# Column sums ahead of the folds of x, a higher credit cap, an eighth pre-split matrix and loads behind gathers in an attention and two-layer MoE kernel

## The chip, the cores and the metric

The kernel runs on one core of a Trainium2 chip. The metric is the time on the device in microseconds, as the median of three executions. TensorE (PE) multiplies, VectorE (DVE) and ScalarE (ACT) work on vectors, GpSimd (POOL) does the same more slowly and also issues gathers and scatters, SyncE (SP) issues most of the other DMAs. Each engine works through a queue of its own in order, and semaphores join them. PEld is the loading of weights into TensorE.

## What is computed

Sparse causal attention (8 global keys, a local window of 96) over q, k, v of 2 x 8 x 768 x 64 gives x, 1536 tokens of 512 values. Two mixture-of-experts layers follow, each with 8 experts of 512 x 1024 and 1024 x 512. In the first, each token goes through each expert, weighted by a matrix P that is balanced in eight rounds of row and column sums; in the second each token goes through the one expert that a greedy assignment gives it.

```python
# layer 1
P = np.exp(logits - logits.max())
for _ in range(8):
    P /= P.sum(1, keepdims=True) + 1e-09
    P /= P.sum(0, keepdims=True) + 1e-09
    P *= N / E
for e in range(E):
    out += P[:, e:e + 1] * (np.maximum(x @ w1[e], 0.0) @ w2[e])
# layer 2: each (token, expert) by falling logit, at most N // E tokens an expert
for e in range(E):
    mask = assigned == e
    out[mask] = np.maximum(x[mask] @ w1[e], 0.0) @ w2[e]
```

## The kernel before

**Numbers.** Each float32 matrix is split into an upper and a lower float16 half (`split_hi` L814 on ScalarE, `split_lo` L817 on VectorE), scaled by a power of two from its largest magnitude, and a product is three float16 matmuls (hi x hi, hi x lo, lo x hi; `mm3`, L868 to L870). A matrix is measured in eight pieces of 128x512, by turns on ScalarE (L882) and VectorE (L1197); `settle` joins them (L1204), a small matmul on TensorE spreads the maximum over the partitions (L134), and VectorE turns it into the scale (L122, L140 to L143).

**Stages.** Attention runs first (to about 155 us). Expert 0's first products (`ph`, L868 to L870, evicted by L861 and L862 on ScalarE and L863 on VectorE) start beside it and go on to 197 us. Meanwhile the eight balancing rounds run: on VectorE row sums, L910 to L913, and the column totals over a partition's tokens, pc (L915); on GpSimd `partition_all_reduce`, the sum of pc over the partitions (L917); on VectorE again L918 to L920. Then come expert 0's second products (`expert_out`, L1459, added into acc by L1464 or L1466 on VectorE with factors from the balanced P), and for each further expert the first products in a form with seven products for eight (`hidden`, L1485) and the second products.

**Folds.** That form needs sums and differences of quarters of x. `fold(tb)`, for each of three blocks of tokens, computes them in six GpSimd instructions (L1105 twice, L1111 four times) into a scratch R, which for the first two blocks lies in chunks 4 to 7 and 8 to 11 of acc, for the third in the buffer of weights; then ScalarE and VectorE convert R (L1119, L1120). The folds are traced behind expert 0's first products, but the compiler's scheduler may issue an instruction of GpSimd as early as its operands are there.

**Streams.** In layer 1 the preparation of weights is laid between the products by hand: generators (`maxima`, `weights`, `folds`, the logits) yield the cost of their next piece on ScalarE, VectorE and GpSimd, and `pump`, called after each few matmuls, grants each engine some credit up to `CAPS`; a piece is issued when the credit of each engine is at least its cost or 0.7, whichever is less. From expert 0's second products to the end of layer 1 (`in_order`) each engine's queue follows the order of tracing. `have` pumps without products where a product needs weights that a stream has not issued yet.

**Layer 2's weights.** Its 16 matrices are all measured in layer 1. The first `NPRE` of them (in the order expert 0 first, expert 0 second, expert 1 first, ...) are also split there and stored in DRAM (`pre`, stores at L1343), and layer 2 fetches them, 2 MB each (`fetch`, L1932); the list of jobs is filled by `some(n)`. The others are made in layer 2 (`make`, L1974): eight loads of 256 KB into a ring of five buffers that lies in acc, each followed by L814 and L817.

**Between the layers** the assignment runs in seven rounds, with held-back products (`held`, L1691, added by `flush`, L1704) in TensorE's gaps. At its end the slot table `inv` is computed, acc is stored to DRAM (xg, L1910), and `load_rows` gathers the rows of two experts at a time by three indirect DMAs on GpSimd's queue (L1942); `turn_rows` transposes them (L1953). For each pair of experts there follow first products, `turn_rows` of the next pair, `load_rows` of the one behind it, `fetch_next(4)`, second products, and the scatter of rows (L1914). Loads of `make` are on SP's queue.

`pin` (`tc.keep_in_program_order`) queues an instruction behind the one traced before it on its engine; `tc.issue_after(ins)` queues what its block traces on the engine of `ins` behind `ins`, without waiting for it to finish.

Of the kernel before, what the change touches and what calls it, by code (L numbers as in the profile page):

```python
# [20 lines left out]
P = 128  # L21
# [21 lines left out]
def tile_sparse_attention_moe_moe(ctx, tc, q, k, v, ng, nl, wg1, w11, w12, wg2, w21, w22, out, taps=None):  # L43
# [809 lines left out]
    S2 = cst.tile([P, 2, E, 2], F32)  # L853
    NPRE = 7

# [52 lines left out]
    for it in range(8):  # L908
# [7 lines left out]
        cs = sml.tile([P, E], F32, name="cs")  # L916
        nc.gpsimd.partition_all_reduce(cs, pc, P, bass_isa.ReduceOp.add)  # L917
        nc.vector.tensor_scalar(cs, cs, 1e-9, float(E) / NT, op0=ALU.add, op1=ALU.mult)  # L918
# [175 lines left out]
    def fold(tb):  # L1094
# [8 lines left out]
        for g in range(2):  # L1103
            yield 0, 0, 4.5
            nc.gpsimd.tensor_tensor(R[g], x[:, 0, KH * g:KH * g + KH], x[:, 1, KH * g:KH * g + KH], op=ALU.add)  # L1105
        a11, a21 = R[0][:, :, :HT], R[0][:, :, HT:]
        a12, a22 = R[1][:, :, :HT], R[1][:, :, HT:]
        for o, u, v, op in ((a22, a21, a22, ALU.add), (a21, a11, a21, ALU.subtract), (a11, a22, a11, ALU.subtract),
                            (a12, a12, a11, ALU.subtract)):
            yield 0, 0, 2.5  # L1110
            nc.gpsimd.tensor_tensor(o, u, v, op=op)  # L1111
        yield None
# [249 lines left out]
    for e in range(1, E - 1):  # L1362
        if e != HB:
            jobs.append(("plain", e, 1))
        jobs.append(("fast", e + 1, 0))
        if e in (2, E - 2):
            jobs.append(("gate", HB if e == 2 else E - 1, 1))
        if e in (1, E - 3):
            jobs.append(("back", HB if e == 1 else E - 1, 1))
        some({2: 1, 4: 3, 6: 2}.get(e, 0))  # L1370
        jobs += [pre.pop() for _ in range(PEEKS.get(e, 0))]
# [27 lines left out]

    credit, CAPS = [0.0, 0.0, 0.0], (2.0, 2.0, 2.0)  # L1400
    GROUP, CHUNK, CYCLE = (0.5, 0.5, 0.6, 3), (0.6, 0.5, 1.1, 3), (0.28, 0.32, 0.6, 3)
# [458 lines left out]
    for n in range(1, NC):  # L1860
# [16 lines left out]
    onep = rawp.tile([P, NC, P], F16, name="raw", bufs=2)  # L1877
    h6 = NC // 2
    nc.vector.tensor_tensor(onep[:, :h6], sp[:, :h6, None].to_broadcast([P, h6, P]),
                            ramp[:, None, :].to_broadcast([P, h6, P]), op=ALU.is_equal)  # L1880
# [84 lines left out]
    def make(e, which):  # L1965
# [4 lines left out]
        for a in range(8):  # L1970
            raw = ring[turn_[0] % len(ring)]
            turn_[0] += 1
            c, h = divmod(a, w.shape[1] // 512)
            nc.sync.dma_start(raw, w[c * P:c * P + P, h * 512:h * 512 + 512])  # L1974
            split(raw, S2[:, which, e], t[:, 0, a * 512:a * 512 + 512], t[:, 1, a * 512:a * 512 + 512])
# [86 lines left out]
```

## Time and profile before

| | |
|---|---|
| median of three executions | 1324.1 us (1322.67 to 1326.08) |
| the profiled execution | 1324.13 us, its span 1322.3 us |
| TensorE busy | 1245.2 us, 94% of the span |
| VectorE busy | 889.4 us, 67% |
| ScalarE busy | 754.1 us, 57% |
| GpSimd busy | 207.0 us, 16% |
| mean granted clock of TensorE | 0.984 |
| bytes moved by DMA | 207.19 MB, 157 GB/s |

The profile comes from one execution; times in it are microseconds from the start of its span, means are nanoseconds. A row of the timeline gives start, duration, engine, line, operation, what is written and read with its shape, a count, and in brackets the idle time of the engine before it and what ended that. The granted clock is the share of TensorE's full speed (2.4 GHz) that it was given.

### The profile page before, as it was taken

What the parts mean: (1) busy time and instruction counts of PE and PEld (TensorE: products, weight loads), DVE (VectorE), ACT (ScalarE), POOL (GpSimd) and SP (SyncE); (2) the same over time, 40 slices, a digit from 0 to 9 for tenths busy, and PEclk for the clock granted to TensorE, in tenths of its full rate; (3) what the DMA queues carried; (4) which work ended last, traced back from release to release, by engine and by line L of the source; (5) the groups of instructions that cost most, each with busy time, mean ns of one, the idle gap of its engine ahead of it and who ended that gap; (6) DMA issues with size and microseconds to landing.
All of it is one profiled execution on the core that took longest, in us unless ns stands there. A gap on an engine that the chain in (4) does not pass through costs nothing.

```text
span 1322.3 us, 24576 instructions
## 1 busy us (share of the span) xinstructions
PE 1245.2 (94%) x9465; PEld 819.7 (62%) x9465; DVE 889.4 (67%) x2038; ACT 754.1 (57%) x1507; POOL 207.0 (16%) x264
## 2 busy tenths in 40 slices
PE   6899959999999999999999999999999999969998
PEld 4666424586479547987458547855785444456665
DVE  7866666677647645868757765766766898844771
ACT  5876432487347425657448644744663686734872
POOL 2543620501101100200200110110000000031100
PEclk8999979999999999999999999999999999989999
DMA  9540013475742356636697676235724234166760
GB/s 237 115 119 12 1 32 128 144 253 181 248 139 88 95 164 196 232 122 192 188 314 233 193 226 194 89 102 158 249 85 166 72 132 148 48 243 250 248 208 25
DMA packets 155509, 207.19 MB, mean 157 GB/s; under 512 B 56448, under 2 KB 89216, under 8 KB 154240
## 3 DMA queue, kind: packets, MB, share of 16 engines
q1 hardware_dynamic: 153040, 193.04, 46.1%
q0 software_dynamic: 1920, 6.29, 1.2%
q10 hardware_dynamic: 432, 6.29, 1.2%
q8 instruction: 74, 1.21, 0.4%
q14 instruction: 43, 0.35, 0.1%
HBM read 174.13 MB, written 31.46 MB: 155 GB/s over the span
## 4 chain that ended last, share of the span: by engine, by line
PE 68%; issue 11%; DVE 9%; ACT 6%; POOL 3%; DMA 2%; POOLq 0%; ACTq 0%; DVEq 0%
PE pX L1459 11%; PE pY L1485 10%; PE pX L1485 7%; PE pY L1459 7%; PE py L1691 6%; PE pZ L1459 5%; PE pV L1459 5%; PE pV L1485 4%; PE pZ L1485 3%; PE ph L868 1%; DMA raw<-in_moe_w_dram 1%; PE ph L869 1%; PE ph L870 1%; PE pr L1813 1%; ACT ex L610 1%
## 5 line engine op out<-in xcount | busy, mean ns | idle before, releaser
L1485 PEld LDWEIGHTS <-ws 128*128 128x128 f16 x3528 | 344.0, 98 | 46.8 <-issue 3.8
L1459 PEld LDWEIGHTS <-hslot 128*128 128x128 f16 x1776 | 173.3, 98 | 204.0 <-issue 7.0
L1459 PE MATMUL pX<-wslot,hslot 128*128 128x512 f16 x768 | 175.3, 384 | 2.0 <-DVE wslot L817 2.0
L1485 PE MATMUL pX<-xt,ws 128*128 128x256 f16 x1008 | 124.4, 273 | 1.6 <-ACT pY L1534 1.6
L1485 PE MATMUL pY<-xs,ws 128*128 128x256 f16 x1008 | 125.1, 273 | 0.0
L1691 PE MATMUL py<-wslot,hslot 128*128 128x512 f16 x528 | 121.0, 379 | 0.0
L1506 DVE TENSOR_TENSOR hslot<-relu,hslot 128x512 f16<-128x512 f32 x126 | 91.1, 746 | 42.1 <-ACT relu L1499 41.1
L1283 POOL TENSOR_TENSOR raw<-raw 128x512 f32<-128x512 f32 x14 | 24.9, 1778 | 526.8 <-DVE ws L817 399.9
L1459 PE MATMUL pY<-wslot,hslot 128*128 128x512 f16 x432 | 97.0, 379 | 0.0
L882 ACT ACTIVATE wide<-raw 128x512 bf16<-128x512 f32 x83 | 52.0, 627 | 68.4 <-DMA raw<-in_moe_w_dram 67.9
L817 DVE SCALAR_TENSOR_TENSOR ws<-raw,s,ws 128x512 f16<-128x512 f32 x98 | 77.7, 824 | 15.4 <-ACT ws L814 15.1
L814 ACT ACTIVATE ws<-raw,s 128x512 f16<-128x512 f32 x98 | 65.6, 716 | 37.6 <-POOL raw L1291 18.7
L1691 PEld LDWEIGHTS <-hslot 128*128 128x128 f16 x528 | 49.4, 99 | 60.6 <-issue 8.4
L817 DVE SCALAR_TENSOR_TENSOR w2slot<-raw,S,w2slot 128x512 f16<-128x512 f32 x72 | 51.8, 749 | 27.5 <-ACT w2slot L814 27.1
L868 PE MATMUL ph<-xt,w2slot 128*128 128x192 f16 x256 | 62.5, 246 | 5.3 <-ACT relu L862 4.6
L1197 DVE TENSOR_REDUCE wam<-raw 128x1 f32<-128x512 f32 x84 | 56.8, 678 | 14.2 <-DMA raw<-in_moe_w_dram 14.2
L1459 PE MATMUL pV<-wslot,hslot 128*128 128x512 f16 x288 | 64.7, 379 | 0.0
L1459 PE MATMUL pZ<-wslot,hslot 128*128 128x512 f16 x288 | 64.4, 379 | 0.0
L814 ACT ACTIVATE w2slot<-raw,S 128x512 f16<-128x512 f32 x72 | 49.2, 722 | 24.4 <-DMA raw<-in_moe_w_dram 19.2
L1485 PE MATMUL pY<-xt,ws 128*128 128x256 f16 x504 | 62.8, 273 | 0.0
L870 PE MATMUL ph<-xt,w2slot 128*128 128x192 f16 x256 | 62.7, 246 | 0.0
L869 PE MATMUL ph<-xt,w2slot 128*128 128x192 f16 x256 | 62.7, 246 | 0.0
(339 smaller groups left out, 2387.1 us busy)
## 6 DMA issues: line engine op xcount, KB each, us to landing
raw<-in_moe_w_dram SPq DMA_DIRECT2D x299, 256.0 KB, 3.3
raw<-in_moe_w_dram SPq DMA_DIRECT2D x60, 512.0 KB, 4.9
relu<-in_moe_w_dram SPq DMA_DIRECT2D x85, 256.0 KB, 2.9
pre<-spill SPq DMA_DIRECT2D x56, 256.0 KB, 4.3
w2slot<-pre SPq DMA_DIRECT2D x4, 2048.0 KB, 12.2
hd<-hslot SPq DMA_DIRECT2D x12, 512.0 KB, 6.2
hslot<-hd SPq DMA_DIRECT2D x12, 512.0 KB, 7.2
w2slot<-pre ACTq DMA_DIRECT2D x3, 2048.0 KB, 15.2
```

What stands on the lines that cost most here:

```text
L814: nc.scalar.activation(hi, raw, AF.Copy, scale=s[:, 0:1])
L817: nc.vector.scalar_tensor_tensor(lo, raw, s[:, 0:1], hi, op0=ALU.mult, op1=ALU.subtract)
L868: nc.tensor.matmul(out_, lhs(0, a), rhs(0, a), start=a == 0, stop=False)
L869: nc.tensor.matmul(out_, lhs(0, a), rhs(1, a), start=False, stop=False)
L870: nc.tensor.matmul(out_, lhs(1, a), rhs(0, a), start=False, stop=a == n - 1)
L882: return nc.scalar.activation(t, src, AF.Abs, accum_out=dst)
L1197: nc.vector.tensor_reduce(am[:, a:a + 1], t, axis=AX.X, op=ALU.max, apply_absolute_value=True)
L1283: nc.gpsimd.tensor_tensor(b11, b12, b11, op=ALU.subtract)
L1459: nc.tensor.matmul(flat(ps), h[:, y1, f, t * P:t * P + P], w[:, y2, f, :], start=f == 0 and n == 0, stop=f == FC - 1 and n == 2, skip_grou ...
L1485: nc.tensor.matmul(bank[:, u, :], self.w[:, z1, m, c, u * P:u * P + P], x[:, z2, c], start=first and u == 0 and c == 0 and n == 0, stop=c ...
L1506: nc.vector.tensor_sub(lo, r, hi)
L1691: pin(nc.tensor.matmul(ps, h[:, y1, f, t * P:t * P + P], w[:, y2, f, :], start=f == 0 and n == 0, stop=f == FC - 1 and n == 2))
```

## The change

Five edits. The folds' GpSimd instructions are queued behind the last `partition_all_reduce` (`summed` holds the eighth of the loop). `CAPS` for ScalarE and VectorE rises from 2.0 to 3.0. `NPRE` rises from 7 to 8, with the eighth matrix (expert 3, second weights) taken up with those of expert 6. One held-back accumulate is flushed before the slot table's comparisons. The first five loads of `make` go to GpSimd's queue, behind what is traced there before them; later ones stay on SP's.

```diff
-    NPRE = 7
+    NPRE = 8
...
-        nc.gpsimd.partition_all_reduce(cs, pc, P, bass_isa.ReduceOp.add)
+        summed = nc.gpsimd.partition_all_reduce(cs, pc, P, bass_isa.ReduceOp.add)
...
         for g in range(2):
             yield 0, 0, 4.5
-            nc.gpsimd.tensor_tensor(R[g], x[:, 0, KH * g:KH * g + KH], x[:, 1, KH * g:KH * g + KH], op=ALU.add)
+            with tc.issue_after(summed.ins):
+                nc.gpsimd.tensor_tensor(R[g], x[:, 0, KH * g:KH * g + KH], x[:, 1, KH * g:KH * g + KH], op=ALU.add)
...
             yield 0, 0, 2.5
-            nc.gpsimd.tensor_tensor(o, u, v, op=op)
+            with tc.issue_after(summed.ins):
+                nc.gpsimd.tensor_tensor(o, u, v, op=op)
...
-        some({2: 1, 4: 3, 6: 2}.get(e, 0))
+        some({2: 1, 4: 3, 6: 3}.get(e, 0))
...
-    credit, CAPS = [0.0, 0.0, 0.0], (2.0, 2.0, 2.0)
+    credit, CAPS = [0.0, 0.0, 0.0], (3.0, 3.0, 2.0)
...
     h6 = NC // 2
+    flush(1)
     nc.vector.tensor_tensor(onep[:, :h6], sp[:, :h6, None].to_broadcast([P, h6, P]),
...
             c, h = divmod(a, w.shape[1] // 512)
-            nc.sync.dma_start(raw, w[c * P:c * P + P, h * 512:h * 512 + 512])
+            if turn_[0] <= len(ring):
+                pin(nc.gpsimd.dma_start(raw, w[c * P:c * P + P, h * 512:h * 512 + 512]))
+            else:
+                nc.sync.dma_start(raw, w[c * P:c * P + P, h * 512:h * 512 + 512])
             split(raw, S2[:, which, e], t[:, 0, a * 512:a * 512 + 512], t[:, 1, a * 512:a * 512 + 512])
```

## Rows read from the trace of the kernel before

**Rows 1.** Waits of TensorE, 140 to 215 us: waiter, releaser, us, times, longest.

```profile
PE pg L134 <- DVE wam L1204: 14.7, 1, 14.7
```

**Rows 2.** Timeline of VectorE, 157 to 182 us: start, duration, instruction, idle time before.

```profile
157.64 1.91 DVE L863 TENSOR_TENSOR hslot<-relu,hslot 128x512 f16<-128x512 f32 x1
...
165.73 0.33 DVE L915 TENSOR_REDUCE pc<-Pm 128x8 f32<-128x96 f32 x1
...
178.22 0.17 DVE L918 TENSOR_SCALAR cs<-cs 128x8 f32<-128x8 f32 x1 [8.22 <-POOL cs L917]
...
181.14 0.69 DVE L863 TENSOR_TENSOR hslot<-relu,hslot 128x512 f16<-128x512 f32 x1
```

**Rows 3.** Timeline of GpSimd, 146 to 233 us.

```profile
146.30 4.58 POOL L1105 TENSOR_TENSOR acc<-xt 128x1024 f32<-128x1024 f16 x2 [6.46 <-ACT relu L862]
150.96 5.96 POOL L1111 TENSOR_TENSOR acc<-acc 128x512 f32<-128x512 f32 x4
...
177.76 0.43 POOL L917 PARTITION_ALL_REDUCE cs<-pc  x1 [5.79 <-issue]
...
203.38 0.40 POOL L917 PARTITION_ALL_REDUCE cs<-pc  x1 [2.23 <-DVE pc L915]
206.01 0.40 POOL L917 PARTITION_ALL_REDUCE cs<-pc  x1 [2.24 <-DVE pc L915]
232.44 1.69 POOL L1283 TENSOR_TENSOR raw<-raw 128x512 f32<-128x512 f32 x1 [26.03 <-DVE ws L817]
```

**Rows 4.** Lines L917 and L1283, GpSimd's queue: count, ns min/median/max, first to last start.

```profile
L917 POOLq MODIFY_POOL_CONFIG  x2: 6/6/6, 171.9 to 172.0; - x2
...
L1283 POOLq MODIFY_POOL_CONFIG  x2: 88/88/88, 206.4 to 206.4; - x2
```

**Rows 5.** Timeline of TensorE, 182 to 225 us.

```profile
182.13 0.63 PE L868 MATMUL ph<-xt,wslot 128*128 128x512 f16 x1
...
187.25 0.42 PE L868 MATMUL ph<-xt,wslot 128*128 128x512 f16 x1
...
197.65 10.52 PE L1459 MATMUL pX<-wslot,hslot 128*128 128x512 f16 x48
...
224.20 0.22 PE L134 MATMUL pg<-identh,wam 128*128 128x128 bf16 x1
```

**Rows 6.** Busy time in a stretch: length, PE, PEld, DVE, ACT, POOL, PEclk, DMA.

```profile
182.00:187.20 5.20, 5.15 (x13) 1.90 (x14) 3.59 (x14) 0.98 (x2) 0.80 (x2) 0.50 0.00 0
```

**Rows 7.** Timeline of ScalarE, first conversion of a fold.

```profile
204.18 1.04 ACT L1119 ACTIVATE xs<-acc 128x1024 f16<-128x1024 f32 x1
```

**Rows 8.** Timeline of VectorE, first conversion and the next L1204.

```profile
209.73 1.22 DVE L1120 TENSOR_TENSOR xs<-acc,xs 128x1024 f16<-128x1024 f32 x1
...
219.24 0.15 DVE L1204 TENSOR_REDUCE wam<-wam 128x1 f32<-128x8 f32 x1
```

**Rows 9.** Timeline of TensorE near 743 us, expert 5's second products.

```profile
743.34 3.39 PE L1459 MATMUL pX<-wslot,hslot 128*128 128x512 f16 x8 [1.98 <-DVE wslot L817]
```

**Rows 10.** Timeline of SP's queue, last stores of split matrices in layer 1.

```profile
965.47 9.06 SPq L1343 DMA_DIRECT2D pre<-spill  x4
```

**Rows 11.** The page's groups, layer 2's splits: count, busy us, mean ns, idle before.

```profile
L817 DVE SCALAR_TENSOR_TENSOR w2slot<-raw,S,w2slot 128x512 f16<-128x512 f32 x72 | 51.8, 749 | 27.5 <-ACT w2slot L814 27.1
...
L814 ACT ACTIVATE w2slot<-raw,S 128x512 f16<-128x512 f32 x72 | 49.2, 722 | 24.4 <-DMA raw<-in_moe_w_dram 19.2
```

**Rows 12.** Timeline of ScalarE in layer 2, a split behind its load.

```profile
1199.24 0.72 ACT L814 ACTIVATE w2slot<-raw,S 128x512 f16<-128x512 f32 x1 [7.81 <-DMA raw<-in_moe_w_dram]
```

**Rows 13.** Timeline of TensorE in layer 2, second products of expert 1.

```profile
1203.82 0.39 PE L868 MATMUL py<-w2slot,xt 128*128 128x512 f16 x1 [1.57 <-ACT xt L861]
```

**Rows 14.** Line L1942 (gathers): first; third with its duration in ns; sixth, each to landing.

```profile
DMA to landing us min/median/max: 5.1/5.1/5.1
...
L1942 POOL DMA_INDIRECT raw<-xg,inv x1: 946/946/946, 1171.3 to 1171.3; - x1
...
DMA to landing us min/median/max: 4.4/4.4/4.4
...
DMA to landing us min/median/max: 3.7/3.7/3.7
```

## What is expected, and why

> **What bounds the kernel now.** TensorE is busy for 94% of the span by the page's first part, so I read its waits, stage by stage; a wait of another engine costs nothing until TensorE stands behind it. The slices show two dips, one a seventh of the way in and one at the start of layer 2. The largest wait of all stands in the first: 14.7 us, once, for a reduce on VectorE [rows 1]. That reduce (L1204) is not slow. It stands in VectorE's queue behind L918, the first step after a column sum, and L918 waits for GpSimd: VectorE has the column totals pc at 165.73 + 0.33 = 166.06 us, yet L918 runs at 178.22 [rows 2]. GpSimd's timeline tells why: from 146.30 on it works through the folds of x, and the first sum starts at 177.76, after a gap of 5.79 us that no instruction explains [rows 3]. Two changes of GpSimd's configuration stand at the head of that gap, at 171.9 and right behind the last fold; two more, at 206.4, right behind the last sum [rows 4]. I read the 5.8 us as the price of such a change. After its wait TensorE runs 12 matmuls from 182.13 to 187.25, 0.427 us each, where 48 later ones start over 10.36 us, 0.216 each [rows 5]: the granted clock from 182.0 to 187.2 is 0.50 [rows 6], its lower level of 1.2 GHz, behind an idle stretch. That is 2.5 us more.
>
> **Part 1, sums ahead of folds.** The six GpSimd instructions of each of three folds now queue behind the eighth sum. One fold costs 4.58 + 5.96 = 10.5 us of GpSimd [rows 3]; none of it is removed.
>
> What the sums gain. The configuration change shows no wait of its own, so it should go in when GpSimd's last attention work is done, before 146.30, and be over when pc comes. pc itself comes earlier: an L863 beside a fold took 1.91 us, one without 0.69 [rows 2]. Some seven operations of VectorE ahead of pc are stretched like that, 8.5 us at 1.22 each; not all are on the chain to pc, so I take 5: first sum at 161 (bounds 158 and 166). Seven intervals follow. A clean one is 206.01 - 203.38 = 2.63 us; as they ran, 206.01 - 177.76 = 28.25 us, 4.04 each [rows 3], because VectorE works on expert 0 between them. So the last sum ends, 0.4 us after its start, between 179.8 and 189.7. I take 185; with pc still at 166 the far end is 195.
>
> What TensorE gains. Its matmul L134 behind L1204 no longer waits: 14.7, and 2.5 of the clock, together 17.2 us. Expert 0's second products start at 197.65 - 17.2 = 180.4, and the next L134 is reached at 224.20 - 17.2 = 207.0 [rows 5].
>
> What is late next: that same next L134. The folds now start behind the last sum, and behind them, in the queues of ScalarE and VectorE, stand the conversions L1119 and L1120, the measurements of the next weights and their L1204. The chain from the end of the last sum: 5.8 for changing the configuration back (26 us of idle GpSimd covered it before [rows 3]); 4.58 and three quarters of 5.96, together 9.05, until half of R is ready [rows 3]; 1.04 for L1119 [rows 7]; 1.22 for L1120 [rows 8]; then the rest of the measurements. That rest took 8.4 us before, from the end of L1120 at 210.95 to the end of L1204 at 219.39 [rows 8], with waits for TensorE in it; I put its lower bound at 5 (an estimate: four reduces of 0.7 and one more load) and take 6.5. Sum 23.6, so L1204 comes at 208.6 and TensorE waits 1.6 us, after which I charge 1.6 of lower clock: the 8 matmuls behind a wait of 1.98 took 3.39 us, 0.42 each instead of 0.216 [rows 9]. Gain 224.2 - 208.6 - 1.6 = 14.0 us. Ends: 17.2 if the last sum ends by 183; with a last sum at 195 and the longer rest, L1204 at 220.5 and a gain of 2.1.
>
> Who else is behind the folds: the evictions of expert 0 (L1464) into acc, of which chunks 4 to 11 are the folds' scratch. Five banks stand between a product and the next one in its bank, five times 5.18 us, cover enough. GpSimd's subtractions for expert 1 come after 185 + 5.8 + 26 = 217, where the shifted kernel wants them at 232.44 - 15.6 [rows 3], the same.
>
> The page "SBUF — State Buffer" of the Trainium skill (section "Who interferes with whom") says that GpSimd, and a VectorE operation with two SBUF inputs, hold one port pair in turn, the second blocked until the first is through. The 1.91 against 0.69 agrees, and it speaks against the folds' new place, since L1120 has two such inputs: rival C.
>
> **Part 2, caps 2.0 to 3.0.** A stream that had to wait may now issue about 1 us more on ScalarE and VectorE in a row. In the long middle of layer 1 TensorE has one wait for weights, 1.98 us and 1.6 of clock [rows 9]. The change may remove it or make another: a gain or a loss of 3.6. I take 0, since no row leans either way.
>
> **Part 3, the eighth matrix (expert 3, second weights) split in layer 1.** Layer 1 gets 8 x 0.722 us on ScalarE and 8 x 0.749 on VectorE [rows 11], four loads and eight stores on SP's queue; its measuring was there before. The last job of this stream ended its stores at 974.5, four of them over 9 us [rows 10]; eight more end at about 995 (a matrix less if the pace of the end is quicker, more if the stores wait), where expert 7's logits are closed and any delay is TensorE's. Cover: ScalarE idles 43% of the span. Cost 0 to 4; I take 1.
>
> In layer 2 the same 5.8 and 6.0 us go. There ScalarE waited 7.81 us for one of this matrix's loads [rows 12], with the relu of expert 1 queued behind it, and TensorE lost 1.57 us [rows 13]: gain 1.6 (0 to 2). The loads of (4,0) behind it don't split sooner, their slot comes free only after the first pair's products. In exchange a fetch of 2 MB stands on SP's queue, wanted only by the second pair's outputs; the loads queued behind it wait for ring buffers anyway.
>
> **Part 4, the first five ring loads on GpSimd, behind the gathers.** Before, SP issued them together with the first gather, which landed after 5.1 us; the third landed after 4.4, the sixth after 3.7 [rows 14]. TensorE starts layer 2 when the third is in: 0.7 (0 to 1.4). The loads cost GpSimd's queue five issues, about 0.95 us each by the gathers [rows 14], and the fourth group of gathers is queued behind them with two pairs of experts as cover. The earlier flush moves one accumulate of 0.7 us ahead of the slot table; the index comes later by as much, but the gather waits longer for the last store of acc: 0.
>
> **Sum.** 14.0 + 0 - 1 + 1.6 + 0.7 = 15.3. The profiled execution took 1324.13 us (span 1322.3), the median of the runs is 1324.1. I predict 1308.8.
>
> **Rivals.**
> A, the whole 17.2: the sums run densely and end by 183, the fold chain is ready before TensorE. For it: 2.63 us once VectorE has no other work. Against: expert 0's work lies between them until TensorE has it done. 1324.1 - 17.2 - 1.3 = 1305.6, and 1302 if the wait for weights goes too.
> B, late sums: VectorE's queue is in order, and the splits of expert 0's second weights fall between the sums; or the configuration change waits with the first sum. Last sum at 190 to 195, L1204 at 213.6 to 218.6, gains 9.0 to 4.0 and 1.3: 1314 to 1319. For it: the mean of 4.04.
> C, the folds hold VectorE: two L1120 on the chain, each longer by 1.22 (as L863 was) or by a fold operation of 2.3: L1204 at 211.0 to 213.2, 1311 to 1313.
> D, the other side: the sums end where they did, at 206.4, because VectorE gives them no earlier turns. L1204 comes at 230.0, 5.8 behind TensorE's 224.2, plus 1.6 of clock, less 1.3: 1330. It decides from a last sum later than about 200. Against: pc is there at 166.
> E, the streams suffer: longer bursts and the eighth matrix make two waits more like that of [rows 9], 7 us: 1316.
> F, the edges don't change the order on the chip, or TensorE finds another wait of 14 us in that place: layer 2 alone remains, 1322.
>
> **How the numbers follow.** Forecast 0.45 (1304 to 1313), A 0.19, B 0.14, C 0.09, E 0.05, D 0.04, F 0.04. The range 1300 to 1319 leaves out D, F and the far ends of the others. A change under 0.3% (4 us) can't be told from none here. Faster by more: the forecast, A, B, C and E without their edges, 0.89; within it: F and the edges, 0.06; slower: D and a worse E, 0.05.
>
> **What would show it.** In the changed profile: no wait of 14.7 us at L134; the configuration change at about 140 and no gap ahead of the first sum at about 161; the last sum at 185; folds from 191 on; a wait of 0 to 3 us at the second L134 near 207; the clock at its upper level from 167 to 200; 64 splits in layer 2 instead of 72, none ahead of expert 1's relu, and no gap before its outputs; the first gather landing in under 4 us. I am wrong if the sums end after 195, if the second L134 waits more than 8 us, or if TensorE's waits in the middle of layer 1 grow by more than 4 us.

## The result, and the profile after

The changed kernel took 1311.8 us (median of four executions, 1308.0 to 1313.7), the kernel before beside it 1324.95 (1322.7 to 1326.1): a ratio of 0.9899, 95% interval 0.9873 to 0.9926. In a second measurement it took 1308.1 (1307.9 to 1312.2) against 1324.8, ratio 0.9877 (0.9857 to 0.9896). The forecast was 1308.8. The number came out, but by luck: its largest term was some 9 us too high and another some 5 us too low.

Below, a difference in microseconds is (ratio - 1) x 1325. The ratio is not exactly the quotient of the two medians: the difference of the medians lies up to 2 us from it (in e2 -6.9 against -5.0, in e3 +0.8 against +2.1).

In the changed kernel's lines, L1105 of before is L1106, L1111 is L1113, L1119 and L1120 are L1121 and L1122, L1197 and L1204 are L1199 and L1206, L1459 and L1485 are L1461 and L1487, L1942 is L1945. Its profiled execution has a span of 1311.9 us. The waits of TensorE from 140 to 250 us (what waited, for what, us in total, times, longest), to be held against [rows 1]:

```profile
PE pg L134 <- DVE wam L1206: 7.5, 3, 4.4
```

One wait of 14.7 has become three, of 2.04, 4.42 and 1.04 (2.04, 6.07 and 1.95 in the second profiled execution), and TensorE's timeline shows where (start, duration, instruction; in brackets the idle time before it and what ended that):

```profile
168.17 0.23 PE L134 MATMUL pg<-identh,wam 128*128 128x128 bf16 x1 [2.04 <-DVE wam L1206]
...
182.87 0.59 PE L1461 MATMUL pX<-wslot,hslot 128*128 128x512 f16 x2
...
211.41 0.29 PE L134 MATMUL pg<-identh,wam 128*128 128x128 bf16 x1 [4.42 <-DVE wam L1206]
211.50 4.05 PE L1461 MATMUL pZ<-wslot,hslot 128*128 128x512 f16 x9
...
240.43 0.23 PE L134 MATMUL pg<-identh,wam 128*128 128x128 bf16 x1 [1.04 <-DVE wam L1206]
```

The second products of expert 0 begin at 182.87, where they began at 197.65 [rows 5]: 14.8 us earlier. The second L134 would have been reached at 211.41 - 4.42 = 206.99, and it runs at 211.41; the nine matmuls behind it start over 211.50 to 215.34, 0.43 us each. That 207.0 was forecast is luck: the lead is 14.8, not 17.2, but this L134 now stands behind 402 of TensorE's product matmuls where it stood behind 414 before. In e1, with the old caps, it stands behind 414, in e2, with the new ones, behind 402, so the caps moved it. GpSimd's timeline and the configuration rows of lines L917 and L1106 on its queue (count, ns, first to last start), beside [rows 3, 4]:

```profile
159.35 0.43 POOL L917 PARTITION_ALL_REDUCE cs<-pc  x1 [19.84 <-DVE pc L915]
...
173.96 0.40 POOL L917 PARTITION_ALL_REDUCE cs<-pc  x1 [2.24 <-DVE pc L915]
182.40 0.40 POOL L917 PARTITION_ALL_REDUCE cs<-pc  x1 [8.04 <-DVE pc L915]
...
188.15 0.40 POOL L917 PARTITION_ALL_REDUCE cs<-pc  x1 [2.24 <-DVE pc L915]
195.52 4.20 POOL L1106 TENSOR_TENSOR acc<-xt 128x1024 f32<-128x1024 f16 x2 [6.96 <-DMA raw<-in_moe_w_dram]
199.79 5.31 POOL L1113 TENSOR_TENSOR acc<-acc 128x512 f32<-128x512 f32 x4
205.06 6.16 POOL L1106 TENSOR_TENSOR acc<-xt 128x1024 f32<-128x1024 f16 x2
```

```profile
L917 POOLq MODIFY_POOL_CONFIG  x2: 11/11/11, 139.5 to 139.5; - x2
...
L1106 POOLq MODIFY_POOL_CONFIG  x2: 88/88/88, 188.5 to 188.5; - x2
```

The configuration is changed at 139.5 and the first sum follows its pc (ready at 159.2) at once; the gap of 5.8 us is hidden. Behind the last sum, which ends at 188.55, the change back stands open: the first fold starts 6.96 us later (195.5, where the forecast had 191). The bracket names a load, but the last wait of GpSimd's queue for that fold was over at 188.50, and in e6 and e12 the same gap waits for nothing (`issue`). VectorE's timeline gives the rest of the chain and what spread the sums:

```profile
157.83 0.25 DVE L910 TENSOR_REDUCE rs<-Pm 128x12 f32<-128x96 f32 x1 [0.21 <-ACT Pm L907]
...
174.69 1.28 DVE L817 SCALAR_TENSOR_TENSOR wslot<-raw,s,wslot 128x1024 f16<-128x1024 f32 x1
...
180.08 1.21 DVE L817 SCALAR_TENSOR_TENSOR wslot<-raw,s,wslot 128x1024 f16<-128x1024 f32 x1
...
204.87 4.37 DVE L1122 TENSOR_TENSOR xs<-acc,xs 128x1024 f16<-128x1024 f32 x2 [10.69 <-ACT xs L1121]
...
211.20 0.16 DVE L1206 TENSOR_REDUCE wam<-wam 128x1 f32<-128x8 f32 x1
```

Four splits of expert 0's second weights, of 1.21 to 1.28 us, and four L863 of 0.69 stand between the fifth sum and the sixth: 8.4 us from start to start instead of 2.63. Then VectorE idles 10.69 us for the fold, converts its two halves in 4.37, and the reduce that TensorE waits for comes at 211.20.

Where the time comes from can be read by numbering TensorE's product matmuls (`ph`, `py`, `pX`, `pY`, `pZ`, `pV`; 7275 in each trace) in order of their starts, and taking the start of the n-th in the kernel before less its start in the other kernel. The columns after `before` are these leads in us (`after` and `again` are the two profiled executions of the changed kernel, e1 to e12 the experiments below). Three cautions: the first row is already apart by up to 1.3 from attention alone, where the order of pieces differs a single row can be off by 3, and a column is one execution, which need not be a typical one (that of `after` is the slowest of its four, those of e2 and e11 are the fastest of their five).

```
    n  before  after again    e1    e2    e3    e4    e5    e6    e7    e8   e10   e11   e12
  200   160.5    1.2   1.0   1.3   0.4   0.5   0.4   1.3   0.4   0.6   1.2   0.5  -0.1   0.6
  300   199.6   14.8  16.3  14.9  -0.1   1.0   0.7  16.6  11.3  15.9  14.8   0.7  11.4  15.9
  416   224.7    7.7   8.5  11.0  -0.1   1.0   0.7  16.6  11.3   7.8   6.6   0.8  11.4  11.7
  540   251.5    6.5   6.3   9.3  -0.1   1.0   0.7  11.4  11.3   6.0   1.9   0.8  11.4   9.6
 2520   542.4    5.8   5.7   8.1  -0.7   1.0   0.7   7.9  10.6   5.3   3.4   0.8  10.8   9.0
 3960   740.3    8.8   8.7   8.4   2.2   1.2   0.4  10.3  13.3   8.3   2.8   0.8  13.8  12.0
 4000   751.6   12.8  12.6   8.1   6.2   1.3   1.0  14.3  17.2  12.2   6.7   0.8  17.7  15.9
 5540  1000.3   11.5  11.8   8.4   5.3   1.2   1.1  13.4  16.4  11.3   5.7   0.8  16.8  15.0
 5700  1044.7   11.6  13.2   6.6   6.7   0.3   1.0  13.1  17.8  12.7   7.2  -0.2  18.2  14.9
 6115  1160.6   11.8  13.3   6.6   6.8   0.4   1.0  13.2  17.9  12.9   7.2  -0.1  18.4  15.1
 6140  1178.9   12.7  14.5   5.5   7.3  -1.0   2.1  14.6  18.9  10.8   8.5   1.4  19.0  16.6
 6320  1195.4   12.7  14.4   5.5   7.3  -1.0  -5.1  14.6  18.9  10.8   8.5   1.0  19.0  16.6
 6362  1206.7   15.0  16.7   7.3   8.2   1.3  -4.3  16.9  21.2  13.1  10.8   3.3  21.2  18.9
 6780  1255.3   14.6  17.3   7.4   8.6   0.3  -4.4  16.7  21.0  12.5  10.3   2.7  20.5  17.8
 6900  1270.5   10.6  16.4   6.9   8.7   0.2  -5.0  16.5  19.3  12.3  10.2   2.5  19.6  18.0
```

In the changed kernel 14.8 us are won ahead of expert 0's second products, 8.3 of them are given back by 250 us, some 5 to 7 come in the rest of layer 1, 1 at the first gather, 2.3 in the first pair of layer 2. In the profiled execution 4.4 are lost again near 1250; in the second one they are not. The middle, waits of TensorE from 255 to 1010 us, has nothing above 1.2 us left (the longest five lines; the kernel before had single waits of 1.98, 1.87, 1.62, 1.44 and 1.42 there):

```profile
PE pg L994 <- DVE xp L986: 1.2, 3, 0.5
PE pg L134 <- DVE gam L1040: 1.1, 1, 1.1
PE pg L1071 <- DVE hslot L1508: 1.1, 1, 1.1
PE pg L1071 <- DVE L L1092: 1.1, 1, 1.1
PE pg L134 <- DVE pjm L974: 1.0, 1, 1.0
```

### The profile page after: what moved, and what is told of

Its sections match the earlier page's. It is cut to its first block, busy times and chain, and to the rows that moved or that the text cites. A ratio compares the mean times of both kernels' runs of the same rounds, so it can differ in the third digit from the quotient of the medians.

```text
span 1311.9 us, 24611 instructions
## 1 busy us (share of the span) xinstructions
PE 1250.9 (95%) x9465; PEld 824.3 (63%) x9465; DVE 886.0 (68%) x2038; ACT 754.7 (58%) x1507; POOL 211.4 (16%) x269
## 3 DMA queue, kind: packets, MB, share of 16 engines
q8 instruction: 74, 1.21, 0.4%
## 4 chain that ended last, share of the span: by engine, by line
PE 61%; issue 9%; DVE 6%; ACT 3%; DMA 2%; POOL 2%; POOLq 0%; ACTq 0%
PE pX L1461 10%; PE pY L1487 10%; PE py L1693 7%; PE pX L1487 7%; PE pY L1461 6%; PE pZ L1461 4%; PE pV L1461 4%; PE pV L1487 4%; PE pZ L1487 3%; DMA raw<-in_moe_w_dram 2%; DVE hslot L1508 2%; PE pr L1815 1%; DVE xt L1805 1%; PE px L979 1%; POOL out_dram L1917 1%
## 5 line engine op out<-in xcount | busy, mean ns | idle before, releaser
L1487 PEld LDWEIGHTS <-ws 128*128 128x128 f16 x3528 | 344.1, 98 | 45.8 <-issue 2.9
L1461 PEld LDWEIGHTS <-hslot 128*128 128x128 f16 x1776 | 173.4, 98 | 202.4 <-issue 5.4
L1461 PE MATMUL pX<-wslot,hslot 128*128 128x512 f16 x768 | 173.7, 382 | 0.0
L1487 PE MATMUL pY<-xs,ws 128*128 128x256 f16 x1008 | 125.3, 273 | 1.0 <-DVE pZ L1567 1.0
L1487 PE MATMUL pX<-xt,ws 128*128 128x256 f16 x1008 | 124.0, 273 | 0.3 <-ACT pY L1536 0.3
L1508 DVE TENSOR_TENSOR hslot<-relu,hslot 128x512 f16<-128x512 f32 x126 | 95.5, 782 | 30.8 <-ACT relu L1501 30.5
L1285 POOL TENSOR_TENSOR raw<-raw 128x512 f32<-128x512 f32 x14 | 22.8, 1631 | 514.6 <-DVE ws L817 251.1
L1461 PE MATMUL pY<-wslot,hslot 128*128 128x512 f16 x432 | 96.8, 379 | 0.0
L817 DVE SCALAR_TENSOR_TENSOR ws<-raw,s,ws 128x512 f16<-128x512 f32 x98 | 77.0, 810 | 14.0 <-ACT ws L814 14.0
L868 PE MATMUL ph<-xt,w2slot 128*128 128x192 f16 x256 | 63.9, 252 | 6.9 <-ACT relu L862 5.6
L1199 DVE TENSOR_REDUCE wam<-raw 128x1 f32<-128x512 f32 x84 | 56.9, 678 | 19.6 <-DMA raw<-in_moe_w_dram 19.6
L1461 PE MATMUL pZ<-wslot,hslot 128*128 128x512 f16 x288 | 67.0, 387 | 0.0
L817 DVE SCALAR_TENSOR_TENSOR w2slot<-raw,S,w2slot 128x512 f16<-128x512 f32 x64 | 46.0, 748 | 27.8 <-ACT w2slot L814 25.4
L1461 PE MATMUL pV<-wslot,hslot 128*128 128x512 f16 x288 | 64.6, 379 | 0.0
L869 PE MATMUL ph<-xt,w2slot 128*128 128x192 f16 x256 | 63.8, 250 | 0.0
L870 PE MATMUL ph<-xt,w2slot 128*128 128x192 f16 x256 | 63.8, 250 | 0.0
L1487 PE MATMUL pY<-xt,ws 128*128 128x256 f16 x504 | 62.4, 273 | 0.0
L1487 PE MATMUL pV<-xs,ws 128*128 128x256 f16 x504 | 61.9, 273 | 0.0
```

The costliest lines, as they stand in the source:

```text
L817: nc.vector.scalar_tensor_tensor(lo, raw, s[:, 0:1], hi, op0=ALU.mult, op1=ALU.subtract)
L868: nc.tensor.matmul(out_, lhs(0, a), rhs(0, a), start=a == 0, stop=False)
L869: nc.tensor.matmul(out_, lhs(0, a), rhs(1, a), start=False, stop=False)
L870: nc.tensor.matmul(out_, lhs(1, a), rhs(0, a), start=False, stop=a == n - 1)
L1199: nc.vector.tensor_reduce(am[:, a:a + 1], t, axis=AX.X, op=ALU.max, apply_absolute_value=True)
L1285: nc.gpsimd.tensor_tensor(b11, b12, b11, op=ALU.subtract)
```

## The experiments

Each kernel ran beside the kernel before; the line numbers are those of the changed kernel where nothing else is said.

| kernel | what | median, us | ratio to before (95%) | difference, us |
|---|---|---|---|---|
| after | all parts | 1311.8 | 0.9899 (0.9873 to 0.9926) | -13.4 |
| after, again | all parts | 1308.1 | 0.9877 (0.9857 to 0.9896) | -16.3 |
| e1 | part 1 alone | 1319.2 | 0.9959 (0.9942 to 0.9977) | -5.4 |
| e2 | part 2 alone | 1318.4 | 0.9962 (0.9948 to 0.9975) | -5.0 |
| e3 | part 3 alone | 1326.1 | 1.0016 (0.9999 to 1.0032) | +2.1 |
| e4 | part 4 alone | 1331.3 | 1.0055 (1.0041 to 1.0068) | +7.3 |
| e10 | parts 3 and 4 | 1322.9 | 0.9989 (0.9972 to 1.0005) | -1.5 |
| e7 | all but the loads of part 4 | 1311.1 | 0.9895 (0.9879 to 0.9911) | -13.9 |
| e5 | all, first fold converted later | 1309.8 | 0.9882 (0.9862 to 0.9901) | -15.6 |
| e6 | all, first fold ahead of the sums | 1305.0 | 0.9850 (0.9830 to 0.9871) | -19.9 |
| e12 | all, two of the first fold's six instructions ahead | 1306.5 | 0.9859 (0.9823 to 0.9894) | -18.7 |
| e11 | e6 with the loads on SP | 1307.5 | 0.9868 (0.9850 to 0.9886) | -17.5 |
| e8 | all, caps of 4 | 1315.6 | 0.9936 (0.9915 to 0.9957) | -8.5 |

### e1, part 1 alone

The edit is the one of `summed` and `issue_after` in the change's diff, nothing else.

> Part 1 alone: the kernel before with only the folds queued behind the last column sum. The forecast's own sum gives it 14.0 us, so 1310 to 1311 against 1325. Theory now, read from the changed kernel's trace: TensorE is 14.8 us ahead when it begins the second product of expert 0, gives 7.1 back at the second L134 (a wait of 4.4 us, the last sum at 188.5, then the lower clock) and 1.2 at the third, so 6 to 7 us remain at 260 us and at the end: 1318 to 1319. If the middle of layer 1 gains only because it starts earlier, and not because of the caps, this kernel shows 1312 to 1313 instead, with no wait for weights near 740 us.

Measured: -5.4 us, and the lead at n = 540 is 9.3, of which 6.9 are there at the end. The rival that the middle gains by starting earlier is out: between n = 540 and 5540 this kernel loses 0.9, and it still waits for weights near 740. Part 1 is worth 5 to 6 us, not 14.

The way there is not the expected one. The second L134 waits 3.70 us, the granted clock from 213.20 to 216.60 is 0.58, and the third L134 doesn't wait at all. VectorE shows why: here the reduce for the third L134 stands ahead of both conversions of the third fold,

```profile
231.82 0.15 DVE L1206 TENSOR_REDUCE wam<-wam 128x1 f32<-128x8 f32 x1
...
237.49 1.65 DVE L1122 TENSOR_TENSOR xs<-ws,xs 128x1024 f16<-128x1024 f32 x1 [0.57 <-ACT xs L1121]
```

while in the changed kernel, with the higher caps, it stands behind them:

```profile
239.09 1.21 DVE L1122 TENSOR_TENSOR xs<-ws,xs 128x1024 f16<-128x1024 f32 x1
240.22 0.15 DVE L1206 TENSOR_REDUCE wam<-wam 128x1 f32<-128x8 f32 x1
```

So the sums alone bring a lead of 9.3 at n = 540, and with the caps beside them 6.5 and 6.3. (Parts 3 and 4 change nothing there: e10 stays at 0.7 to 0.8 from n = 300 to 5540.)

### e2, part 2 alone

```
-    credit, CAPS = [0.0, 0.0, 0.0], (2.0, 2.0, 2.0)
+    credit, CAPS = [0.0, 0.0, 0.0], (3.0, 3.0, 2.0)
```

> Part 2 alone: the kernel before with caps of 3.0, 3.0, 2.0. The forecast gave it 0 (1325, ends 1321 and 1329). Theory now: between 540 and 745 us of the changed kernel TensorE gains 6.6 us in three steps (2.1, 1.8 and 3.8) at places where the kernel before waits for weights or logits; if the caps do this, 1318 to 1319 with the wait of 1.98 us for wslot gone. If that gain belongs to the eighth matrix or to the earlier start, 1325.

Measured: -5.0 us. The lead grows from -0.1 at n = 540 to 5.3 at 5540, as it does in the whole change (6.5 to 11.5), and TensorE's waits from 255 to 1010 us are those of the changed kernel, 8.6 us in all, the longest this one:

```profile
PE pg L134 <- DVE gam L1040: 1.1, 1, 1.1
```

So the gain in the middle of layer 1 belongs to the caps. The 1.98 us at 743 [rows 9] is gone, and with it four waits of 1.4 to 1.9 us that the forecast didn't look at. TensorE's waits there add up to 12.4 us before, with new small ones counted to 8.6 in the changed kernel; the 3.8 between and the 1.6 of lower clock behind the wait at 743 make 5.4, which is what the lead shows. Alone, the caps make no wait at the second or third L134; beside the sums they cost the 3 us of lead that e1 shows.

### e3, part 3 alone

```
-    NPRE = 7
+    NPRE = 8
-        some({2: 1, 4: 3, 6: 2}.get(e, 0))
+        some({2: 1, 4: 3, 6: 3}.get(e, 0))
```

> Part 3 alone: the eighth matrix split in layer 1 instead of layer 2. The forecast: 1 us lost at the end of layer 1, 1.6 gained at the wait for the split of expert 1's activations, together 1324.4. Theory now: 1 to 1.4 lost before the end of layer 1, 2.3 gained in the first pair of layer 2, so 1324 (1323 to 1325), 64 splits in layer 2. If the middle's gain is this part's, 1318.

Measured: +2.1 us, the interval just reaching none; the median of 1326.1 is above the 1323 to 1325 expected. The lead tells its parts: 0.9 lost between n = 5540 and 5700, 1.4 at the first gather (it landed after 6.2 us here, 5.1 before), 2.3 gained in the first pair of layer 2, 1.1 lost behind it. The first loss has its place. VectorE, ScalarE and TensorE (lines of the kernel before):

```profile
1014.75 1.41 DVE L817 SCALAR_TENSOR_TENSOR spill<-raw,S,spill 128x512 f16<-128x512 f32 x2
```

```profile
1016.85 1.47 ACT L1799 ACTIVATE xt<-raw,rw 128x1408 bf16<-128x1408 f32 x1 [0.86 <-DVE raw L1776]
```

```profile
1020.83 0.40 PE L1813 MATMUL pr<-xt,Bz 128*32 128x512 bf16 x4 [0.95 <-ACT xt L1797]
```

The last two splits of the eighth matrix run on VectorE at the start of the assignment, ahead of a copy (L1776) that ScalarE's L1799 needs; ScalarE waits 0.86 us, and TensorE behind it 0.95, which neither does before. Their stores end at 1016.7. In e10, also without the higher caps, these two splits stand at 1015.27, and the wait is there again, 0.94. In the changed kernel the last six stores of this line are issued by 975.6:

```profile
963.24 12.39 SPq L1345 DMA_DIRECT2D pre<-spill  x6
```

That is 41 us sooner with as many matrices, and no such wait: with the caps the eighth matrix costs no wait in layer 1.

### e4, part 4 alone

```
+    flush(1)
...
+            if turn_[0] <= len(ring):
+                pin(nc.gpsimd.dma_start(raw, w[c * P:c * P + P, h * 512:h * 512 + 512]))
+            else:
+                nc.sync.dma_start(raw, w[c * P:c * P + P, h * 512:h * 512 + 512])
```

> Part 4 alone: the first five ring loads behind the gathers on GpSimd's queue, and one accumulate flushed earlier. The forecast: 0.7 us, 1324.3 (0 to 1.4). Theory now, from the changed kernel: the wait of 7.4 us ahead of the first transposes of layer 2 falls to 5.4 and 1.1 to 1.9 us are gained: 1323 to 1324. Against: here 72 splits remain, and the split of expert 3's second weights waits for loads that are now issued some 10 us later with the relu of expert 1 queued behind, so 1 to 3 us may be lost again: 1325 to 1327.

Measured: +7.3 us, outside what either reading expected. The gather did its part: the lead rises by 1.1 at n = 6140. Then 7.2 us go at n = 6320. ScalarE and TensorE there:

```profile
1183.87 0.48 ACT L862 ACTIVATE relu<-ph 128x384 f32<-128x384 f32 x1
1194.37 0.72 ACT L814 ACTIVATE w2slot<-raw,S 128x512 f16<-128x512 f32 x1 [10.02 <-DMA raw<-in_moe_w_dram]
```

```profile
1198.37 0.59 PE L868 MATMUL py<-w2slot,xt 128*128 128x512 f16 x1 [6.02 <-ACT relu L862]
```

ScalarE waits 10.02 us for a load that is now issued behind nine gathers; in its queue the relu of expert 1 stands behind that split, and TensorE waits 6.02 us for it. The mechanism is the one of [rows 12, 13], four times as dear.

### e7 and e10, parts 3 and 4 together

e7 is the changed kernel with `nc.sync.dma_start` for all ring loads; e10 is the kernel before with both diffs above.

> The changed kernel with all ring loads back on SP's queue (part 4 undone, the flush kept). By itself part 4 cost 6.0 us on the kernel before; the four parts alone sum to -6.2 us where the whole change gives -13.1. Theory: the cost was the eighth matrix's: its splits, with the relu of expert 1 queued behind them, waited 10 us for loads issued behind nine gathers; with the eighth matrix out of layer 2 nothing urgent waits for these loads, and what remains of part 4 is the gather landing earlier, 0.7 to 1.9 us. So this kernel is 0.7 to 1.9 slower than the changed one: 1312.5 to 1313.7. Rival: part 4 costs 6 in any company and two others of the parts reinforce each other: 1305 to 1307.

> The kernel before with parts 3 and 4 alone (the eighth matrix split in layer 1, the ring loads behind the gathers and the earlier flush). By themselves they cost 0.8 and 6.0 us. Theory: the 6.0 is the wait of the eighth matrix's splits in layer 2 for loads now issued behind nine gathers, and with that matrix out of layer 2 it is gone; together they give -1 to +1: 1324 to 1326, with no wait over 1 us at py in the first pair. Rival: the costs add to 6.8: 1332.

Measured: e10 -1.5 us where the two alone add to +9.4; it has no wait of TensorE between 1185 and 1210. So the cost of part 4 is owed to the eighth matrix in layer 2, and part 3 takes it away. What then is left of part 4 shows at n = 6140 and in the first gather (to landing, us), first in e7, then in e6, which has these loads on GpSimd:

```profile
DMA to landing us min/median/max: 7.2/7.2/7.2
```

```profile
DMA to landing us min/median/max: 3.7/3.7/3.7
```

The wait of TensorE for the first rows is 8.87 us in e7, 6.9 to 7.8 in e1, e3 and before, 7.5 in e11, and 5.3 to 5.4 in every kernel that has the loads behind the gathers. Between n = 6115 and 6140 that is a lead of 0.9 to 1.5 us with part 4, and from 0.6 down to -2.1 without it. The earlier flush, which has no run of its own, doesn't bring it: e7 and e11 keep the flush and stand at -2.1 and 0.6. The medians don't resolve it: e7 stands at -13.9 between the two measurements of the whole change, -13.4 and -16.3, and its 1311.1 is below the 1312.5 to 1313.7 expected.

### e5, the conversion behind the reduce

```
         yield None
+        if tb == 0:
+            yield from pause(42)
         if tb not in XS:
```

> The changed kernel, but the conversion of the first fold (L1119 and L1120 of before) is traced some 40 us of products later, so that in VectorE's queue the L1204 of the next weights stands ahead of it instead of behind; what GpSimd does is untouched. Theory: the second L134 waits only because its reduce is queued behind that conversion (last sum 188.5, configuration, fold, conversions of 2.2 us each). Then the wait of 4.4 us near 211 is gone, TensorE reaches that L134 at about 207 and keeps its lead of 14.8 us past 215 at the upper clock: 7.1 us more than the changed kernel there, and 5 to 8 at the end: 1304 to 1307 against 1311.8. Rival 1: the evictions into the folds' scratch, or the conversions themselves, hold TensorE by its banks just as long, only later: 1310 to 1312 with a wait of 3 us or more before 235. Rival 2: the earlier start is taken back in the middle by the delivery of weights: the lead at 260 us is 12 to 14 us, but below 10 at 500: 1309 to 1311.

Measured: -15.6 us, 1309.8 where 1304 to 1307 was expected; it lies between the two measurements of the changed kernel, so the time shows no gain. By the lead the theory's first half holds. VectorE's reduce comes at 198.87 while the conversion still waits for the fold until 205 (lines two higher than in the changed kernel):

```profile
198.87 0.16 DVE L1208 TENSOR_REDUCE wam<-wam 128x1 f32<-128x8 f32 x1
205.13 4.37 DVE L1124 TENSOR_TENSOR xs<-acc,xs 128x1024 f16<-128x1024 f32 x2 [6.10 <-ACT xs L1123]
```

The second L134 doesn't wait, and the lead stays at 16.6 us past 224. So the conversion in front of the reduce was the cause of the second wait. But the third L134 now waits 3.34 instead of 1.04: its reduce at 233.65 stands behind three splits (L817) that take 4.69 us together beside the last folds. The lead falls to 11.4 by n = 540, and 3.5 more go by 542 us, much as rival 2 has it, most of them in one wait of 3.09 us at 431.94 for logits (L1003), which no row ties to the folds. Taking one consumer out of the fold chain's way showed the next.

### e6 and e12, part of the folds ahead of the sums

e6 leaves the whole first fold in its old place, e12 only its first two instructions (L1106).

```
-            with tc.issue_after(summed.ins):
+            with tc.issue_after(summed.ins) if tb else nullcontext():
```

(in e6 at both places, in e12 at the first)

> The changed kernel, but the first of the three folds keeps its old place ahead of the sums; the other two stay behind them. Theory: that fold runs from about 146 to 157, the configuration change of 5.8 us follows, the first sum comes at 162.5 instead of 159.35; the conversions of the first fold find their operand ready, so the wait of 4.4 us at the second L134 is gone, but the first L134 waits 3 us longer (5 instead of 2). Sum: 7 less, 3 to 4.5 more: 1308 to 1309. Rival: the fold's port takes VectorE's time as before (L863 1.9 instead of 0.69) and the sums come another 3 us later: 1311 to 1313. In both the two conversions of the first fold show 1.3 us each where GpSimd stands still, and 2 where it works.

> The changed kernel, but the first two of the first fold's six GpSimd instructions (4.58 us) keep their old place ahead of the sums; its other four and the other folds stay behind. With the whole fold ahead, the second wait was gone and the first L134 waited 3.96 instead of 2.04, because fold and configuration together end at 162, 2.7 us after the totals. Theory: half a fold ends at 150.5, the configuration is over by 156.3 and the first sum stays at 159.3, so the first L134 waits 2.0; behind the last sum (188.2 to 188.6) only 7 us of configuration and three of the four short instructions (4 us) stand ahead of the conversions, so the reduce for the second L134 ends at about 207, where TensorE arrives: a wait of 0 to 1. Lead of 14.8 to 16.3 at 260 us against 11.3: 1301 to 1304. Rival: the chain behind the last sum is no shorter because the conversions then meet the second fold's instructions on the port, and the second wait is 2 to 4 us: 1306 to 1309.

Measured in e6: -19.9 us, 1305.0, the fastest kernel of the study: 6.5 us ahead of the first measurement of the changed kernel, and 3.6 ahead of the second, whose interval overlaps with its own. GpSimd, VectorE and TensorE:

```profile
145.86 4.58 POOL L1106 TENSOR_TENSOR acc<-xt 128x1024 f32<-128x1024 f16 x2 [6.46 <-ACT relu L862]
150.52 5.96 POOL L1113 TENSOR_TENSOR acc<-acc 128x512 f32<-128x512 f32 x4
162.01 0.43 POOL L917 PARTITION_ALL_REDUCE cs<-pc  x1 [5.53 <-issue]
```

```profile
198.03 4.29 DVE L1122 TENSOR_TENSOR xs<-acc,xs 128x1024 f16<-128x1024 f32 x2 [0.33 <-ACT xs L1121]
...
204.27 0.16 DVE L1206 TENSOR_REDUCE wam<-wam 128x1 f32<-128x8 f32 x1
```

```profile
170.83 0.29 PE L134 MATMUL pg<-identh,wam 128*128 128x128 bf16 x1 [3.96 <-DVE wam L1206]
```

The fold fits into GpSimd's idle stretch, the first sum comes at 162.01 (162.5 expected), the first wait of TensorE is 3.96 instead of 2.04, and it is the only one: the reduce for the second L134 comes at 204.27, and the lead of 11.3 us stays where it was through n = 540. The expected 1308 to 1309 were too careful, since the third wait went as well, and they were counted from 1311.8, the slower of the two measurements.

e12 gave -18.7 us, 1306.5 where 1301 to 1304 was expected, by its interval not to be told from e6. Its first sum stays at 159.94 and its first wait at 2.04, but the second is 2.34 and the third 1.86: the rival's mechanism. Of the chain behind its last sum, which ends at 189.3, the change of configuration took 7.35 us and the two conversions 4.37; the theory had put the former at 7 and gave the latter no stretch.

### e8, a still higher cap

The caps are `(4.0, 4.0, 2.0)`.

> The changed kernel with caps of 4.0, 4.0, 2.0. Theory: the caps' 6.9 us came from waits for weights and logits in the middle of layer 1 that are now gone (2.0 at wslot, 1.6 and 1.4 at pieces of logits and spilled factors, with the clock behind them); what is left there adds up to some 3 us, so a higher cap gains 0 to 2: 1310 to 1312. Rival: longer bursts on VectorE make new waits: 1313 to 1317.

Measured: -8.5 us, so 5 to 8 slower than with caps of 3 (the interval overlaps with that of the first measurement, not with that of the second): the rival. By the lead, 4.6 of it are lost before n = 540. The second and third L134 wait 5.39 and 2.78 us there, and the granted clock behind them is 0.50 and 0.60 for 4.3 us each; with caps of 2 (e1) the third doesn't wait, with caps of 3 it waits 1.04 and 1.95. Waits from 255 to 1010 us add up to 11.3 where 8.6 was left with caps of 3, one of them of 2.4. That fits the rival's reason, that longer bursts put more in front of what TensorE waits for.

### The changed kernel again, and e11

> The changed kernel itself, run beside the two below on one chip, as the comparison for them and as a second trace of its layer 2. 1311 to 1313. In its first trace TensorE lost 4.4 us between 1240 and 1260, behind one load that came 1.5 us late and a lower clock afterwards. Theory: that belongs to that execution, and here the first and second products of layer 2 lose under 2 us there. Rival: it belongs to the kernel and shows again.

> The changed kernel with the first fold ahead of the sums and all ring loads on SP's queue. With the changed kernel's other folds, putting these loads back moved the median by -0.8 us, where the wait for the first gathers grew by 2.7 us in its profile. Theory: part 4 is worth 2 to 3 us at the first gather in company of the eighth matrix, and the medians of the earlier pair hid it: 1306.5 to 1308. Rival: it is worth nothing, since the later loads get those microseconds back at the end of layer 2, where splits pace TensorE: 1304 to 1305.5.

The second measurement of the changed kernel gave 1308.1, 3 below the range expected. Its trace loses 0.9 between n = 6780 and 6900 where the first lost 4.0. In the first, splits near 1249 fall back by 1.5 us against those of the kernel before, TensorE waits 3.31 at 1252.00, and the granted clock from 1230 to 1260 is 0.89; in the second the longest wait there is 1.92 and the clock 1.00. So that loss belongs to an execution, not to the change. e11 is 2.4 us slower than e6, with intervals that overlap; this leans to the theory that the gathers are worth something, and doesn't show it.

## Why the prediction came out, point by point

**The bound, and part 1's first half: right.** The wait of 14.7 us was GpSimd's order, the configuration change went in at 139.5 (140 forecast), the first sum came at 159.35 (161), and TensorE began expert 0's second products at 182.87 (180.4). The 2.5 us between lie at the first L134: the forecast let it run without a wait, but its L1206 stands in VectorE's queue behind the second sum, and TensorE still waits 2.04 us. Behind that wait the granted clock from 168.60 to 172.00 was 0.52 in one execution of the changed kernel and 1.00 in the other, after the same 2.04:

```profile
168.60:172.00 3.40, 3.40 (x10) 1.14 (x8) 2.83 (x17) 0.15 (x1) 0.40 (x1) 0.52 0.00 0
```

```profile
168.60:172.00 3.40, 3.40 (x17) 1.55 (x16) 2.73 (x16) 1.44 (x2) 0.51 (x2) 1.00 0.00 0
```

(length, busy time of PE, PEld, DVE, ACT and POOL, granted clock, DMA share.) That is the difference of 1.5 between leads of 14.8 and 16.3. The forecast wanted the upper clock from 167 to 200; it came in one of the two.

**Part 1's second half: the right chain, too small.** The chain from the end of the last sum to the end of the reduce was forecast at 23.6 us and took 211.36 - 188.55 = 22.8: 6.96 for the configuration (5.8 put), 8.26 until half of R is ready (9.05), then 1.1 for L1121, and 4.37 for both L1122 and 2.1 for what was left, where one L1120 of 1.22 and a rest of 6.5 were put. Its start was late: the last sum ended at 188.55, not 185, inside the bounds of 179.8 and 189.7 and for the reason of rival B, four splits of weights between two sums. TensorE waited 4.42 (6.07 in the second execution) instead of 1.6, and the nine matmuls behind it took 4.05 us at a granted clock of 0.50 from 211.40 to 215.40. From n = 300 to 416 the lead falls by 7.1, where the forecast charged 3.2.

**What the forecast left out** is the third L134, and that parts 1 and 2 meet there. It asked what is late next, and stopped after one answer; and it sized each part alone. The sums put the conversions of the third fold at 233.69 and 239.09, and the caps trace the reduce behind them: the third L134 waits 1.04 and 1.95 us in the two executions, and 1.2 and 2.2 us of lead go. With the sums alone (e1) it doesn't wait, with the caps alone (e2) it doesn't, with caps of 4 (e8) it waits 2.78. Part 1 alone reached a lead of 14.9, lost 3.9 at the second L134 and 1.7 behind it, and gave 5.4 us in the end (e1) instead of 14.0. This is the term that was mis-sized by most. The forecast also put expert 1's subtractions on GpSimd at 217, with 26 us of folds ahead of them that no row gives (three folds of 10.5 are 31.5); the first ran at 224.70.

**Rival C** (the folds hold VectorE) was a part of this, not a case of its own: L1122 took 2.2 us beside a fold where L1120 took 1.22 [rows 8]. Its numbers, the reduce at 211.0 to 213.2 and 1311 to 1313, were met (211.2 and 1311.8) by a chain that began 3.5 us later and had a shorter rest. The page "SBUF — State Buffer" of the Trainium skill (section "Who interferes with whom") says that GpSimd and such an operation hold the port pair in turn, whoever issues first. The runs agree in both directions: in e6 an L1122 that starts at 226.75, ahead of GpSimd's L1113 at 226.82, takes 1.23 us, and the L1113 takes 2.29 instead of 1.27.

**Part 2: wrong.** The forecast took 0 with 3.6 on either side, because it judged the caps by one wait, that of [rows 9]. The view of TensorE's waits from 255 to 1010 us in the kernel before held four more of 1.4 to 1.9 us, for logits (L1003, L1092) and for a copy of ScalarE (L1534):

```profile
PE pg L992 <- DVE V L1003: 2.9, 2, 1.4
PE pX L1459 <- DVE wslot L817: 2.0, 1, 2.0
PE pg L134 <- DVE L L1092: 1.9, 1, 1.9
PE pX L1485 <- ACT pY L1534: 1.6, 1, 1.6
```

The waits of over 1.2 us all went, smaller ones came, and e2 gives 5.0 alone. Beside part 1 the caps take about 3 of that back at the second and third L134. The bound of 3.6 was worked out from one row where the waits of the stretch should have been summed.

**Part 3: right in size, 20 us late in layer 1.** 1 us at the end of layer 1 was forecast, and 0.95 measured without the higher caps, but at the start of the assignment, behind two splits on VectorE, with stores until 1016.7 (995 forecast); with the caps the wait vanishes. In layer 2 the wait of 1.57 went, and the lead there grows by 2.3 (1.6 forecast). 64 splits of 72 remain, each as long as before [rows 11]; the page's groups:

```profile
L817 DVE SCALAR_TENSOR_TENSOR w2slot<-raw,S,w2slot 128x512 f16<-128x512 f32 x64 | 46.0, 748 | 27.8 <-ACT w2slot L814 25.4
```

**Part 4: right only in company.** 0.7 was forecast, 0.9 to 1.5 came, with a first gather that lands after 3.7 us instead of 5.1. That it would cost without part 3 (7.3 us, e4) could be seen in [rows 12, 13], where ScalarE already waits 7.81 us for one of the eighth matrix's loads, and the forecast, which sized each part by itself, didn't say that this one leans on another.

**The sum.** 14.0 + 0 - 1 + 1.6 + 0.7 was forecast. By the lead of the first trace it was 5.3 for part 1 (6.5 less the 1.2 that were there at n = 200), 5.1 for the rest of layer 1, 1 at the gather and 2.3 in the first pair, less 4.4 that the second trace doesn't lose. An error of 9 us in part 1, some 3 of it owed to the caps, met one of 5 in part 2 and some 2 more in the small terms. That is luck: without the caps, their gain of 5.1 in the middle and their cost of 2.8 ahead of it, the time would have been near 1314 (an estimate, 1311.8 + 5.1 - 2.8); e1 and e10 added, all parts but the caps, give -6.9, or 1318. Both are inside the range, which reached 1319 for rival B.

## What to carry to other kernels

When a wait is taken away by moving work behind something, follow the moved work to each of its consumers in order, not only to the first: here the second wait cost 7 and the third 1 to 2 us with the clock behind them, and keeping just the first fold in the idle 20 us of GpSimd (e6) gave 3.6 to 6.5 back. Before calling a tuning constant neutral, add up all the waits that its streams stand behind, and test edits in the company that they come in: the loads that cost 7 us alone were free, or better, beside the eighth matrix, and the caps that bring 5 us alone took 3 from the sums.

## What the runs showed of the hardware

A change of GpSimd's configuration showed as two short rows (`MODIFY_POOL_CONFIG`, 1 to 88 ns) and a gap behind them: 5.53 to 5.79 us from elementwise work to the first sum, in the seven traces where a fold stands right ahead of it, and more on the way back, 6.79 to 8.01 us from the end of the last sum to the first elementwise instruction, in the nine traces where a fold stands right behind it (6.96 in the changed kernel, 8.01 in e1). Where GpSimd was idle for 19.84 us ahead of the first sum, the gap was hidden. The page "GPSIMD Engine Reference" of the Trainium skill (section "2.1 Instruction dispatch") gives 5.95 us, without an instruction of its own, for the first call after such a change; the way to the sum agrees, the way back is longer.

The same wait of 2.04 us of TensorE was followed by a granted clock of 0.52 in one execution and of 1.00 in another of the same kernel. So what the lower clock costs behind such a wait is a range here, not a number.
